# Backward pass of a sliding-window decode block on one Trainium2 core: 4 KB rows for two weight gradients, and three first loads on Pool's queue

## The chip, the cores and the metric

The kernel runs on one core of a Trainium2 chip. The metric is the time of one execution on the device in microseconds (us); of several runs the median is taken. A core has five engines that run their own instruction streams: PE (TensorE, matrix products and transposes), DVE (VectorE), ACT (ScalarE), POOL (GpSimd) and SP (SyncE, here only an issuer of transfers). Sixteen DMA engines move data between the chip's memory (HBM) and the core's working memory. A transfer is issued by SP or ACT through a hardware queue (q1 for SP, q10 for ACT in the profile), or by POOL through a software queue (q0).

## The reference

The forward function is y = x + attention(norm(x)) + ffn(norm(x)), and the kernel computes y and the gradients of it for a given grad_out. There are 4 sequences with one token each, D = 512.

```python
xn = layernorm(x)                                  # 4 x 1 x 512
q  = xn @ wq                                       # 32 heads of 128
k, v = k_cache[:, :, -1024:], v_cache[:, :, -1024:]  # 8 kv heads, 4 query heads share one
p  = softmax(q k^T / sqrt(128));  o = p v
y  = x + o @ wo + (gelu(xn @ w_gate) * (xn @ w_up)) @ w_down      # F = 1792
outputs: y, dx, dk_cache, dv_cache, dwq, dwo, dw_gate, dw_up, dw_down
```

The cache gradients have all 4096 positions, of which the first 3072 are zero: 50.3 MB of zeros are to be written beside 16.8 MB of dk and dv and 13.9 MB of weight gradients. Two of the outputs matter here: dwo = o^T grad_out (4096 x 512) and dwd = a^T grad_out (1792 x 512), with a the product of gelu and w_up's result. Both are sums over four rows only (the four sequences), so each is a matrix product with a very short inner dimension whose cost is in copying and storing the result. All arrays are bfloat16.

## The kernel before

The kernel has two parts in one instruction stream. The FFN part comes first: w_gate, w_up and w_down are loaded whole; xn and grad_out are transposed; the hidden values hg and hu are computed with xnT (L538 to L543); w_down is transposed on PE in seven steps and multiplied with grad_out to da (L582 to L589); a chain of small DVE operations gives a, dhg and dhu in transposed form; `f_rows` (L615) turns them back into rows (a_r, dhg_r, dhu_r); and the pieces of dwd (`piece_d`, L629), dw_gate and dw_up (`piece_g`, L640) are queued as background work.

The attention part then goes over NT = 4 groups t of two kv heads (eight query heads). `pre(t)` computes do and q of the group from wo and wq, `kv_steps` transposes k or v in eight steps and computes scores, `softmax` and `softmax_d` are chains of small operations whose links are placed between PE work, `odq` computes o (k = 0) and dq (k = 1), `dvdk` queues the pieces of dv and dk, `dw` those of dwo and dwq, and `fin` adds the group's part to y and dx.

The order is written out by hand. Each engine's instructions run in the order in which the program emits them. Background pieces stand in one queue, `bg`, and `tick(n)` emits the next n of them between other work; `link` does the same for the softmax chains. A copy from PE's result memory goes through `evac` (L89), which puts it on ACT or DVE by a running estimate of their load. A piece's last step emits its store on SP.

All stores, and k's and v's loads, are issued by SP, in program order. When SP reaches a store whose data is not ready, it waits, and everything behind it waits as well. The zeros of the cache gradients are stores of a zeroed tile, `ztile`, 1.5 MB each, 32 in all (`zero`, L161). They are placed between the other stores to keep the DMA engines fed: two after the first loads (L168), one after each dv or dk store (L478), single ones in the FFN part (L638, L650), and three ahead of the last group's dv (L706); what is left comes at the end (L727).

Before the change the first transfers are: ACT issues w_gate; SP issues x, grad_out, w_up, w_down (L150), wo and wq of group 0 (`load_w(0, nc.sync)`, L151), k and v of group 0, and then two zero stores. POOL builds the identity, sets `ztile` to zero (L167), builds `sel` (L177) and sets further tiles. POOL issues wo and wq of the later groups.

dwo is made as follows. `dym` (L232) holds grad_out spread by `spread_rows` (L234): four copies of it on 128 rows, in the i-th of which only the rows with row number i modulo 4 are kept. The product of the rows of o (one row for each sequence and query head) with the i-th copy is the block of dwo of query head i: 128 rows by 512. A staging tile holds four such blocks next to each other, and the store writes them as 128 x 4 rows of 512 elements, 1 KB each. dwd goes the same way with chunks of F in place of heads.

Of the kernel before, what the change touches and what calls it, by code (L numbers as in the profile page):

```python
# [9 lines left out]
ACT = mybir.ActivationFunctionType  # L10
ALU = mybir.AluOpType
AX = mybir.AxisListType
FP32 = mybir.dt.float32
BF16 = mybir.dt.bfloat16
P = 128
# [3 lines left out]
def kernel(  # L19
# [28 lines left out]
    nc = tc.nc  # L48

    B, Sq, D = A_x.shape  # L50
# [3 lines left out]
    rep = Hq // G  # L54
# [5 lines left out]
    GP = 2  # L60
# [56 lines left out]
    wo_t, wq_t, k_t, v_t = {}, {}, {}, {}  # L117
    w_pool, kv_pool = {0: w_a}, {0: kv_a}

    def load_w(t, eng=nc.gpsimd):  # L120
        pool = w_pool[t % 2]
        wo_t[t] = pool.tile([P, HG, D], BF16, name="wo_sb", tag="wo")
        eng.dma_start(out=wo_t[t][:], in_=wo_v[t])
        wq_t[t] = pool.tile([P, ND, CW], BF16, name="wq_sb", tag="wq")
        eng.dma_start(out=wq_t[t][:], in_=wq_v[t])

    def load_kv(t, k):
        if t >= NT:
# [18 lines left out]
    make_identity(nc, ident[:])  # L147

    wd_sb = ffn_w.tile([P, NF, D], BF16, name="wd_sb")
    nc.sync.dma_start(out=wd_sb[:], in_=B_w_down.rearrange("(c p) n -> p c n", p=P))  # L150
    load_w(0, nc.sync)  # L151
    for k in range(2):
        load_kv(0, k)

# [10 lines left out]


    nc.gpsimd.memset(ztile[:], 0.0)  # L167
    zero(2)  # L168
    ident_f = const.tile([P, P], FP32, name="ident_f")
    nc.vector.tensor_copy(out=ident_f[:], in_=ident[:])  # L170
# [58 lines left out]


    xnm = const.tile([P, rep, D], BF16, name="xnm")
    dym = const.tile([P, rep, D], BF16, name="dym")  # L232

    def spread_rows(src, dst):  # L234
        ps = ps_w.tile([P, D], FP32, name="row_ps", tag="w")
        nc.tensor.matmul(ps[:], lhsT=sel[:], rhs=src[:], start=True, stop=True)
        for i in range(rep):
            if i % 2:
                nc.scalar.activation(out=dst[:, i, :], in_=ps[:], func=ACT.Copy, scale=msk_i[:, i:i + 1])
            else:  # L240
                nc.vector.tensor_scalar(out=dst[:, i, :], in0=ps[:], scalar1=msk_i[:, i:i + 1], scalar2=None,
                                        op0=ALU.mult)
# [196 lines left out]
    def odq(t, k):  # L439
        pT, blks = st[t][("PT", "dST")[k]], (v_t, k_t)[k]  # L440
        cols = pT[:].rearrange("p j (y s) -> p j s y", s=SL)
        for j in range(JB):
            q, jj = j // JQ, j % JQ
            for g in range(GP):
                nc.tensor.matmul(od_ps[g * 32:g * 32 + B * rep, k, g, :], lhsT=cols[:, jj, g * NQ + q, :],  # L445
                                 rhs=blks[(t, g)][:, j, :], start=(j == 0), stop=(j == JB - 1),
                                 tile_position=(0, g * 32))
        rows = attw.tile([P, GP, Dh], BF16, name="od_r", tag=f"od_r{k}", bufs=2)
        if k == 0:
            nc.vector.tensor_copy(out=rows[:], in_=od_ps[:, k])  # L450
        else:
            nc.scalar.activation(out=rows[:], in_=od_ps[:, k], func=ACT.Copy, scale=scale)
        st[t][("o", "dq")[k]] = rows

    def odT(t, k):
        rows = st[t][("o", "dq")[k]]
# [27 lines left out]
        return made  # L484

    def dw(t):
        o_r, dq_r = st[t]["o"], st[t]["dq"]

        def piece_o(g, i, held):
            if i == 0:  # L490
                held["osb"] = outp.tile([P, rep, D], BF16, name="osb_o", tag="o")
            mps = ps_w.tile([P, D], FP32, name="dwo_ps", tag="w")
            nc.tensor.matmul(mps[:], lhsT=o_r[:, g, :], rhs=dym[:, i, :], start=True, stop=True)  # L493
            evac(held["osb"][:, i, :], mps[:], 512)
            if i == rep - 1:
                r0 = (t * HG + g * rep) * Dh
                store(nc.sync, out_5[r0:r0 + rep * Dh, :].rearrange("(h p) n -> p h n", p=P), held["osb"][:], "rest")

        def piece_q(c2, k, held):
            if k == 0:  # L500
                held["osb"] = outp.tile([P, 2, GP, rep, Dh], BF16, name="osb_q", tag="o")
            ci, i2 = k // 2, k % 2
            c = c2 * 2 + ci
            mps = ps_w.tile([P, 2, GP, Dh], FP32, name="dwq_ps", tag="w")
            for i in range(2):
                nc.tensor.matmul(mps[:, i].rearrange("p g d -> p (g d)"), lhsT=xnm[:, i2 * 2 + i, c * P:(c + 1) * P],  # L506
                                 rhs=dq_r[:].rearrange("p g d -> p (g d)"), start=True, stop=True)
            evac(held["osb"][:, ci, :, i2 * 2:(i2 + 1) * 2, :], mps[:].rearrange("p i g d -> p g i d"), 512)
            if k == 3:
                store(nc.sync, out_4[c2 * 2 * P:(c2 + 1) * 2 * P, t * CW:(t + 1) * CW].rearrange("(c p) j -> p c j", p=P),  # L510
                      held["osb"][:].rearrange("p c g i d -> p c (g i d)"), "rest")

        assert rep == 4
        made = []
        for g in range(GP):
            held = {}
            made.append([lambda g=g, i=i, held=held: piece_o(g, i, held) for i in range(rep)])
        for c2 in range(ND // 2):
            held = {}
            made.append([lambda c2=c2, k=k, held=held: piece_q(c2, k, held) for k in range(4)])  # L520
        return made
# [17 lines left out]
    for wi, wsb in enumerate((wg_sb, wu_sb)):  # L539
        for fc in range(NF):  # L540
            for c in range(ND):
                nc.tensor.matmul(hg_ps[:, wi, fc, :], lhsT=wsb[:, c, fc * P:(fc + 1) * P], rhs=xnT[:, c, :],
                                 start=(c == 0), stop=(c == ND - 1))  # L543
    spread_rows(dy4, dym)
    hgu = ffn.tile([P, 2, 4 * NF4, B], FP32, name="hgu")
    nc.gpsimd.memset(hgu[:], 0.0)
    nc.vector.tensor_copy(out=hgu[:, :, 0:NF], in_=hg_ps[:])
# [64 lines left out]
    nc.vector.tensor_tensor(out=dhg_f[:], in0=da[:], in1=hu, op=ALU.mult)  # L612
    nc.vector.tensor_tensor(out=by_chunk(dhgT_b), in0=fbi(dhg_f), in1=fbi(gp), op=ALU.mult)

    def f_rows(srcT, nm):  # L615

        ps = ps_w.tile([P, NF4, P], FP32, name="fr_ps", tag="w")
        for f4 in range(NF4):
            nc.tensor.matmul(ps[0:4 * B, f4, :], lhsT=srcT[:, f4].rearrange("p b i -> p (b i)"),
                             rhs=ident[:], start=True, stop=True)  # L620
        rows = const.tile([P, NF4, P], BF16, name=nm)
        nc.gpsimd.memset(rows[:], 0.0)
        evac(rows[0:4 * B], ps[0:4 * B], 512)
        return rows

    acc_sum(0, [(lambda c, fc=fc: wd_sb[:, fc, c * P:(c + 1) * P], aT_b[:, fc // 4, :, fc % 4]) for fc in range(NF)])
    a_r = f_rows(aT_b, "a_r")

    def piece_d(f4, i, n, held):  # L629
        if i == 0:  # L630
            held["osb"] = outp.tile([P, 4, D], BF16, name="osb_d", tag="o")
        mps = ps_w.tile([P, D], FP32, name="dwd_ps", tag="w")
        nc.tensor.matmul(mps[:], lhsT=a_r[:, f4, :], rhs=dym[:, i, :], start=True, stop=True)
        evac(held["osb"][:, i, :], mps[:], 512)
        if i == n - 1:
            store(nc.sync, out_8[4 * f4 * P:(4 * f4 + n) * P, :].rearrange("(h p) n -> p h n", p=P),
                  held["osb"][:, 0:n, :], "rest")
            zero(f4 == 1)  # L638

    def piece_g(s_r, og, c, i, held):  # L640
# [11 lines left out]
    for f4 in range(NF4):  # L652
        held = {}
        n = min(4, NF - 4 * f4)
        for i in range(n):
            bg.append(lambda f4=f4, i=i, n=n, held=held: piece_d(f4, i, n, held))
    df_ps = ps_a.tile([P, ND, B], FP32, name="df_ps", tag="S")
    edge = dict(lhsT=ztile[0:1, 0:P], rhs=ztile[0:1, 0:ND * B])
# [131 lines left out]
```

## Time and profile before

| What | Value |
|---|---|
| Runs | 285.17, 285.85, 285.30 us; median 285.3 |
| Profiled execution | 285.17 us, span of its instructions 283.4 us |
| TensorE clock granted, mean | 0.894 |
| PE, DVE, ACT, POOL busy | 201.9, 161.0, 116.9, 29.7 us |
| DMA packets | 23981, 112.12 MB, mean 396 GB/s |
| Read from and written to HBM | 30.68 and 81.01 MB |

The page of the profile gives busy time for each engine, the span in 40 slices with a digit for the busy share of each slice, the DMA queues with packets and bytes, the chain of waits that ended last, and the costliest groups of instructions. A row of a group or of the timeline reads: start and length in us, engine, line, operation, the tile written and the tiles read, their shapes, and in brackets how long the engine sat idle before and what ended that. SPq is SyncE's instruction stream. A DMA view can be asked for any stretch of time and then gives packets and bytes of each queue in it.

### The profile page before, as it was taken

What the parts mean: (1) busy time and instruction counts of PE and PEld (TensorE: products, weight loads), DVE (VectorE), ACT (ScalarE), POOL (GpSimd) and SP (SyncE); (2) the same over time, 40 slices, a digit from 0 to 9 for tenths busy, and PEclk for the clock granted to TensorE, in tenths of its full rate; (3) what the DMA queues carried; (4) which work ended last, traced back from release to release, by engine and by line L of the source; (5) the groups of instructions that cost most, each with busy time, mean ns of one, the idle gap of its engine ahead of it and who ended that gap; (6) DMA issues with size and microseconds to landing.
All of it is one profiled execution on the core that took longest, in us unless ns stands there. A gap on an engine that the chain in (4) does not pass through costs nothing.

```text
span 283.4 us, 6845 instructions
## 1 busy us (share of the span) xinstructions
PE 201.9 (71%) x2970; PEld 138.0 (49%) x2970; DVE 161.0 (57%) x310; ACT 116.9 (41%) x219; POOL 29.7 (10%) x32
## 2 busy tenths in 40 slices
PE   0455998898888799999894899999996997200000
PEld 0444676665556764676652567665555743100000
DVE  7756556476847555768562677667774387800000
ACT  2041484561146177644371564447660387200000
POOL 8400000043000700001600000220000000000000
PEclk9999599799999999999999599999997799955555
DMA  7999999999999999999999999999999979999993
GB/s 266 391 356 420 424 408 404 432 420 364 384 426 409 402 418 418 404 420 417 406 388 416 423 426 424 401 418 394 384 407 388 433 286 425 424 397 404 425 420 153
DMA packets 23981, 112.12 MB, mean 396 GB/s; under 512 B 1664, under 2 KB 10384, under 8 KB 15504
## 3 DMA queue, kind: packets, MB, share of 16 engines
q1 hardware_dynamic: 22160, 103.56, 90.4%
q0 software_dynamic: 1632, 6.29, 5.7%
q10 hardware_dynamic: 160, 1.84, 1.7%
q8 instruction: 23, 0.38, 0.5%
q14 instruction: 6, 0.05, 0.0%
HBM read 30.68 MB, written 81.01 MB: 394 GB/s over the span
## 4 chain that ended last, share of the span: by engine, by line
PE 34%; issue 19%; DMA 17%; DVE 10%; POOL 5%; ACT 3%; POOLq 0%; ACTq 0%; DVEq 0%; SPq 0%
DMA out_dram<-stg_dv 10%; DMA wq_sb<-in_A_wq_dram 7%; PE kv_ps L472 7%; PE T_ps L274 6%; PE od_ps L445 5%; PE S_ps L340 4%; PE dwq_ps L506 2%; DVE dS_s L362 2%; POOL ztile L167 2%; PE pT_ps L274 2%; PE dwo_ps L493 2%; DVE T_sb L98 1%; PE acc_ps L251 1%; DVE P_s L362 1%; PE woT_ps L274 1%
## 5 line engine op out<-in xcount | busy, mean ns | idle before, releaser
L98 DVE COPY T_sb<-T_ps 128x1024 bf16<-128x1024 bf16 x64 | 44.1, 689 | 25.3 <-PE T_ps L274 25.3
L97 ACT CAST stg_dv<-kv_ps 128x512 bf16<-128x512 f32 x52 | 28.4, 589 | 26.6 <-PE kv_ps L472 26.0
L97 ACT CAST stg_dk<-kv_ps 128x512 bf16<-128x512 f32 x51 | 28.4, 588 | 25.8 <-PE kv_ps L472 11.2
L472 PE MATMUL kv_ps<-qmr,dS_s 128*128 128x512 bf16 x64 | 22.9, 396 | 2.3 <-ACT stg_dk L97 1.4
L274 PE MATMUL T_ps<-ident,vb 128*128 128x128 bf16 x256 | 20.7, 228 | 4.6 <-ACT stg_dk L97 4.2
L324 POOL TENSOR_TENSOR domr<-r,msk 128x1024 bf16<-128x1024 bf16 x4 | 7.6, 1889 | 153.1 <-DVE r L321 126.3
L274 PEld LDWEIGHTS <-vb 128*128 128x128 bf16 x256 | 17.5, 102 | 9.1 <-issue 7.2
L472 PE MATMUL kv_ps<-domr,P_s 128*128 128x512 bf16 x64 | 21.6, 386 | 0.1
L274 PE MATMUL T_ps<-ident,kb 128*128 128x128 bf16 x256 | 19.5, 219 | 0.0
L274 PEld LDWEIGHTS <-kb 128*128 128x128 bf16 x256 | 16.5, 98 | 4.3 <-issue 0.9
L97 ACT CAST osb_q<-dwq_ps 128x512 bf16<-128x512 f32 x26 | 15.1, 586 | 7.2 <-PE dwq_ps L506 5.3
L97 ACT CAST osb_g<-dwg_ps 128x512 bf16<-128x512 f32 (+1 forms) x26 | 12.8, 538 | 10.0 <-PE dwg_ps L645 6.8
L97 ACT CAST osb_o<-dwo_ps 128x512 bf16<-128x512 f32 x24 | 13.8, 585 | 4.7 <-PE dwo_ps L493 3.8
L98 DVE COPY wgT<-wgT_ps 128x1024 bf16<-128x1024 bf16 x14 | 9.6, 689 | 7.9 <-PE wgT_ps L274 7.8
L98 DVE CAST stg_dv<-kv_ps 128x512 bf16<-128x512 f32 x12 | 8.2, 687 | 8.6 <-PE kv_ps L472 8.4
L340 PE MATMUL S_ps<-T_sb,qm 128*32 128x256 bf16 x128 | 12.7, 386 | 0.5 <-DVE T_sb L98 0.5
L98 DVE COPY woT<-woT_ps 128x1024 bf16<-128x1024 bf16 x16 | 11.0, 687 | 3.2 <-PE woT_ps L274 2.8
L340 PE MATMUL S_ps<-T_sb,dom 128*32 128x256 bf16 x128 | 12.7, 387 | 0.0
L98 DVE CAST stg_dk<-kv_ps 128x512 bf16<-128x512 f32 x13 | 8.6, 688 | 6.9 <-DMA out_dram<-stg_dv 5.8
L493 PE MATMUL dwo_ps<-dym,od_r 128*128 128x512 bf16 x32 | 11.9, 390 | 0.2
L506 PE MATMUL dwq_ps<-od_r,xnm 128*128 128x256 bf16 x64 | 11.8, 274 | 0.1
L98 DVE COPY wqT<-wqT_ps 128x1024 bf16<-128x1024 bf16 x16 | 10.6, 686 | 2.2 <-PE wqT_ps L274 2.1
(186 smaller groups left out, 363.9 us busy)
## 6 DMA issues: line engine op xcount, KB each, us to landing
out_dram<-ztile SPq DMA_DIRECT2D x32, 1536.0 KB, 18.6
kb<-in_A_k_cache_dram SPq DMA_DIRECT2D x8, 1024.0 KB, 13.4
vb<-in_A_v_cache_dram SPq DMA_DIRECT2D x8, 1024.0 KB, 18.6
out_dram<-stg_dv SPq DMA_DIRECT2D x8, 1024.0 KB, 15.5
out_dram<-stg_dk SPq DMA_DIRECT2D x8, 1024.0 KB, 16.1
out_dram<-osb_o SPq DMA_DIRECT2D x8, 512.0 KB, 19.2
out_dram<-osb_q SPq DMA_DIRECT2D x8, 512.0 KB, 11.9
out_dram<-osb_g SPq DMA_DIRECT2D x8, 448.0 KB, 8.5
```

Of the source, the lines that this page charges most:

```text
L97: return nc.scalar.copy(out=out, in_=in_)
L98: return nc.vector.tensor_copy(out=out, in_=in_)
L167: nc.gpsimd.memset(ztile[:], 0.0)
L251: nc.tensor.matmul(ps[:, c, :], lhsT=lf(c), rhs=rhs, start=(k == 0), stop=(k == len(terms) - 1))
L274: nc.tensor.transpose(ps[:, i, :], a, ident[:])
L324: nc.gpsimd.tensor_tensor(out=mr[:].rearrange("p g q d -> p (g q) d"), in0=r4[:, k, :].unsqueeze(1).broadcast_to([P, SL, Dh]), in1=msk[:]. ...
L340: nc.tensor.matmul(ps[b * RB:(b + 1) * RB, :], lhsT=zt[:, b * GP + g, c0:c0 + RB], rhs=T_sb[:].rearrange("p (x b) -> p b x", b=B)[:, b, :] ...
L362: nc.vector.scalar_tensor_tensor(out=out[:], in0=src[:].unsqueeze(2).broadcast_to([P, WQ, B]), scalar=rr[:, 0:1], in1=mskb[:].unsqueeze(1) ...
L445: nc.tensor.matmul(od_ps[g * 32:g * 32 + B * rep, k, g, :], lhsT=cols[:, jj, g * NQ + q, :], rhs=blks[(t, g)][:, j, :], start=(j == 0), st ...
L472: nc.tensor.matmul(mps[:].rearrange("p q d -> p (q d)"), lhsT=src[:, j * P:(j + 1) * P], rhs=mr[:, g].rearrange("p q d -> p (q d)"), start ...
L493: nc.tensor.matmul(mps[:], lhsT=o_r[:, g, :], rhs=dym[:, i, :], start=True, stop=True)
L506: nc.tensor.matmul(mps[:, i].rearrange("p g d -> p (g d)"), lhsT=xnm[:, i2 * 2 + i, c * P:(c + 1) * P], rhs=dq_r[:].rearrange("p g d -> p ...
```

## The change

The change has these parts.

- dwo: the four masked copies of grad_out are replaced by one unmasked, `dyr`. The mask goes to the other factor: after o of a group is there (`odq(t, 0)`), two POOL products write `o_s`, four copies of o's rows in which the i-th keeps the rows of head i. The product for step i then takes every fourth column of `o_s`, starting at i, so that its 128 result rows are the rows 4p + i of the 512 rows of dwo. With the four steps next to each other in the staging tile, a partition holds four rows of dwo that follow each other in HBM, and the store writes 128 rows of 4 KB.
- dwd: the same with `a_s` in place of `a_r`, made by `f_rows(..., spread=True)` in four masked copies that alternate between DVE and ACT. The last chunk of two blocks now takes four steps of 64 rows where it had two of 128: 16 products in place of 14.
- w_down is issued by POOL, behind the identity and ahead of the zeroing of `ztile`; wo and wq of group 0 are issued by POOL behind that zeroing. SP goes from w_up straight to k and v of group 0 and the two zero stores.
- POOL sets `a_s` to zero (128 x 2048) in place of `a_r` (128 x 512).

The zero stores keep their places in the program.

```diff
-    def load_w(t, eng=nc.gpsimd):
+    def load_w(t):
         ...
-        eng.dma_start(out=wo_t[t][:], in_=wo_v[t])
+        nc.gpsimd.dma_start(out=wo_t[t][:], in_=wo_v[t])
         ...
-        eng.dma_start(out=wq_t[t][:], in_=wq_v[t])
+        nc.gpsimd.dma_start(out=wq_t[t][:], in_=wq_v[t])
...
-    nc.sync.dma_start(out=wd_sb[:], in_=B_w_down.rearrange("(c p) n -> p c n", p=P))
-    load_w(0, nc.sync)
+    nc.gpsimd.dma_start(out=wd_sb[:], in_=B_w_down.rearrange("(c p) n -> p c n", p=P))
     for k in range(2):
         load_kv(0, k)
...
     nc.gpsimd.memset(ztile[:], 0.0)
+    load_w(0)
     zero(2)
...
-    dym = const.tile([P, rep, D], BF16, name="dym")
-
-    def spread_rows(src, dst):
+    dyr = const.tile([P, D], BF16, name="dyr")
+    msk_r = const.tile([P, rep], BF16, name="msk_r")
+    nc.vector.tensor_copy(out=msk_r[:], in_=msk_i[:])
+
+    def spread_rows(src, dst, masked=True):
         ps = ps_w.tile([P, D], FP32, name="row_ps", tag="w")
         nc.tensor.matmul(ps[:], lhsT=sel[:], rhs=src[:], start=True, stop=True)
+        if not masked:
+            evac(dst[:], ps[:], 512)
+            return
...
         st[t][("o", "dq")[k]] = rows
+        if k == 0:
+            o_s = attw.tile([P, GP, rep, Dh], BF16, name="o_s", tag="o_s", bufs=2)
+            for g in range(GP):
+                nc.gpsimd.tensor_tensor(out=o_s[:, g], in0=rows[:, g].unsqueeze(1).broadcast_to([P, rep, Dh]),
+                                        in1=msk_r[:].unsqueeze(2).broadcast_to([P, rep, Dh]), op=ALU.mult)
+            st[t]["os"] = o_s
...
-            nc.tensor.matmul(mps[:], lhsT=o_r[:, g, :], rhs=dym[:, i, :], start=True, stop=True)
+            nc.tensor.matmul(mps[:], lhsT=o_s[:, g].rearrange("p r d -> p (r d)")[:, i:rep * Dh:rep], rhs=dyr[:],
+                             start=True, stop=True)
...
-                store(nc.sync, out_5[r0:r0 + rep * Dh, :].rearrange("(h p) n -> p h n", p=P), held["osb"][:], "rest")
+                store(nc.sync, out_5[r0:r0 + rep * Dh, :].rearrange("(p i) n -> p (i n)", i=rep),
+                      held["osb"][:].rearrange("p i n -> p (i n)"), "rest")
...
-    spread_rows(dy4, dym)
+    spread_rows(dy4, dyr, masked=False)
...
-    def f_rows(srcT, nm):
+    def f_rows(srcT, nm, spread=False):
         ...
+        if spread:
+            rows = ffn.tile([P, NF4, 4, P], BF16, name=nm)
+            nc.gpsimd.memset(rows[:], 0.0)
+            for i in range(4):
+                if i % 2:
+                    nc.scalar.activation(out=rows[0:4 * B, :, i, :], in_=ps[0:4 * B], func=ACT.Copy,
+                                         scale=msk_i[0:4 * B, i:i + 1])
+                else:
+                    nc.vector.tensor_scalar(out=rows[0:4 * B, :, i, :], in0=ps[0:4 * B],
+                                            scalar1=msk_i[0:4 * B, i:i + 1], scalar2=None, op0=ALU.mult)
+            return rows
...
-    a_r = f_rows(aT_b, "a_r")
+    a_s = f_rows(aT_b, "a_s", spread=True)
...
+        m = n * P // 4
         mps = ps_w.tile([P, D], FP32, name="dwd_ps", tag="w")
-        nc.tensor.matmul(mps[:], lhsT=a_r[:, f4, :], rhs=dym[:, i, :], start=True, stop=True)
-        evac(held["osb"][:, i, :], mps[:], 512)
-        if i == n - 1:
-            store(nc.sync, out_8[4 * f4 * P:(4 * f4 + n) * P, :].rearrange("(h p) n -> p h n", p=P),
-                  held["osb"][:, 0:n, :], "rest")
+        nc.tensor.matmul(mps[0:m], lhsT=a_s[:, f4].rearrange("p i f -> p (i f)")[:, i:n * P:4], rhs=dyr[:],
+                         start=True, stop=True)
+        evac(held["osb"][0:m, i, :], mps[0:m], 512)
+        if i == 3:
+            store(nc.sync, out_8[4 * f4 * P:(4 * f4 + n) * P, :].rearrange("(p i) n -> p (i n)", i=4),
+                  held["osb"][0:m].rearrange("p i n -> p (i n)"), "rest")
             zero(f4 == 1)
...
-        for i in range(n):
+        for i in range(4):
             bg.append(lambda f4=f4, i=i, n=n, held=held: piece_d(f4, i, n, held))
```

More of the change, by code (lines that the diff above doesn't have):

```diff
@@ L486, in dw @@
     def dw(t):
-        o_r, dq_r = st[t]["o"], st[t]["dq"]
+        o_s, dq_r = st[t]["os"], st[t]["dq"]
         def piece_o(g, i, held):
```

## The prediction

> **What bounds the kernel now.** I read the page first, for what the DMA engines do, then the queues' rows for single stretches of time, then SyncE's own waits and the timeline of the first 45 us, because most of the change lies there, and last the chain.
>
> Four lines of the page:
>
> ```profile
> DMA  7999999999999999999999999999999979999993
> DMA packets 23981, 112.12 MB, mean 396 GB/s; under 512 B 1664, under 2 KB 10384, under 8 KB 15504
> q1 hardware_dynamic: 22160, 103.56, 90.4%
> q0 software_dynamic: 1632, 6.29, 5.7%
> ```
>
> The DMA engines are busy from the second slice to the last, with one dip (the slice with a 7, around 229 us) and a slow start. 112 MB have to be moved whatever the order, so the time is the bytes' own time plus every microsecond in which the queue is empty. A compute engine counts only where its lateness empties the queue. q0, the queue of Pool's transfers, moved 6.29 MB in 5.7% of 283.4 us, which is 389 GB/s; its 4 KB packets are the only ones of that size in this trace.
>
> The DMA view of three stretches, 13 to 17 us (only 1 KB rows of w_down and wo), 24 to 30 us (only 8 KB rows of k and v), and 69 to 72.5 us (Pool's wo beside k and v):
>
> ```profile
> DMA packets 1380, 1.40 MB, mean 350 GB/s; under 512 B 13, under 2 KB 1380, under 8 KB 1380
> ...
> DMA packets 353, 2.50 MB, mean 417 GB/s; under 512 B 44, under 2 KB 44, under 8 KB 50
> ...
> q1 hardware_dynamic: 124, 0.89, 66.0%
> q0 software_dynamic: 109, 0.45, 36.2%
> ```
>
> Rows of 1 KB move at 350 GB/s, rows of 8 KB at 417. In the third stretch 0.89 MB of 8 KB rows are 109 packets, and q0 has 109 of 4 KB (0.45 MB): the two queues take turns packet by packet, so Pool's queue gets a third of the bandwidth beside 8 KB rows.
>
> SyncE's waits, and the timeline rows of PE, SyncE and ScalarE that decide the start:
>
> ```profile
> SPq L103 <- ACT osb_d L97: 16.5, 4, 13.7
> 18.00 1.89 PE L274 MATMUL wdT_ps<-ident,wd_sb 128*128 128x128 bf16 x16 [2.98 <-DMA wd_sb<-in_B_w_down_dram]
> 19.09 1.27 SPq L103 DMA_DIRECT2D out_dram<-ztile  x2
> 31.18 0.57 ACT L97 CAST a_r<-fr_ps 16x512 bf16<-16x512 f32 x1 [2.29 <-PE fr_ps L619]
> 36.11 2.88 SPq L103 DMA_DIRECT2D out_dram<-osb_d  x2
> ```
>
> PE starts w_down's transposes when w_down lands, at 18.0. SyncE, after two zero stores at 19.1, stands 13.7 us at the first dwd store. Until then the engines live on what was queued: loads of 11.8 MB (w_gate, w_up and w_down 1.84 each, wo and wq 1.05 each, k and v 4.19) and 3.1 MB of zeros. 1 KB rows of dwd first appear between 39 and 40 us, where the rate falls to 333 GB/s from 419 in the three microseconds before. So the queued work ends at about 39.4, 3.3 us after the store was issued: a small margin.
>
> The chain, where it goes through a DMA:
>
> ```profile
> 65.43 19.51 DMA wq_sb<-in_A_wq_dram
> 136.44 19.60 DMA out_dram<-stg_dv
> 228.26 8.36 DMA out_dram<-stg_dv
> ```
>
> Twice compute waits some 20 us for a DMA, which is a queue full of older work. A queue that is late by some time at 85 or 156 us hands its lateness to compute. The third comes after the dip: there compute was late and the queue empty.
>
> **The change, part by part.** The sum is made against the profiled execution, 285.17 us with a span of 283.4; the median of the runs is 285.3, 0.13 higher.
>
> Larger packets. dwd (1.84 MB) and dwo (4.19 MB) go from 1 KB to 4 KB rows on the hardware queue. No such packet is in the trace: 389 GB/s (4 KB on q0) and 417 (8 KB) are the ends, I take 400. From 350, dwd saves 1.84/350 - 1.84/400 = 0.65 us, dwo 1.49 (0.37 a group); the ends are 1.7 and 2.8 for both. w_down and the first wo (2.88 MB) go from 350 to q0's 389: 0.84. wq moved at 388 between 20 and 22 us: 0. Together 3.0 us of DMA time. The Trainium skill, "DMA: Bandwidth & Descriptors" (Why small descriptors are slow), has a fixed overhead of about 3 cycles a packet beside a 32 B beat, from which I estimate 35 beats for 1 KB and 131 for 4 KB, a saving of 6.4%, or 1.6 us on these 8.9 MB. The trace's own rates, 350 against 389 to 417, differ by more, and the sum goes by them.
>
> w_down on Pool. Pool issues it after the identity, at 1.4 us. Its issue with 1792 rows is not shown; wo's (1024 rows) took 0.93 to 1.06 and wq's (512) 0.76, so 1.2 to 1.5. q0 has no packet until 68.9 for an issue begun at 64.4, 4.5 us; so w_down's first packets come at about 6.3. At that time w_gate and w_up, done at 11.3 before, have 5.0 us to go: 9.4 rows of 14 KB for each engine, 0.536 each, 7.5 of them w_up's. In turns, 7.5 of w_down's 28 packets for each engine (0.168 at 389 GB/s) go meanwhile, to 12.6. The other 20.5 take turns with 8 KB rows of k and v, which now follow w_up at once on SyncE's queue (0.314 + 0.168 = 0.482 a turn): 9.9 us, to 22.5. Before, the data was through at 16.5 (11.3 + 1.84/350) and w_down landed at 18.0; the same 1.5 puts landing at 24.0, 6.0 later. Ends: 18 if q0 starts at once and its share beside w_gate and w_up is larger than a turn, 25.5 if some engine lags. The Trainium skill speaks against this edit in the same page's rules: transfers from several issuing engines share the same 16 DMA engines and interleave, so spreading them saves issue time alone. The 109 to 109 packets agree with the interleaving; by the rule the move is worth nothing in bandwidth.
>
> SyncE's queue loses three loads; wo and wq held it 8.61 and 3.57 us there. k, v and the two zeros are issued earlier (zeros at about 8, when Pool's memset of 5.2 us, now behind w_down's issue, ends). All of that lies in a full queue: 0. Pool's later memsets move from 6.5 to about 10, and that of a_s is longer (four times the 0.51 of a_r); PE needs sel at 14.4 before and later now, a_s past 31: 0 while Pool isn't held.
>
> dyr. One copy takes the place of four masked ones that ran one after another (15.06 to 18.04): 2.3 us saved, but then comes the wait for w_down: 0.
>
> a_s. Four copies that alternate between VectorE and ScalarE, some 3.0 us by the dym rows, in place of 0.57. PE's first dwd product, at 32.48, can start at about 34.1: +1.6 on the path to the first store. dwd has 16 products instead of 14; two more of 0.38 and their copies of 0.59 fall behind that store.
>
> o_s. Two Pool products of 128x512 a group; 128x1024 took 1.89, so 0.95 each. Pool is idle for over 25 us before each group's domr, and dwo comes after dk: 0 for themselves. But VectorE's dS_s reads SBUF twice about then (215.72, after od_r at 214.68), and VectorE's identity cast took 5.2 us beside Pool's memset of 5.2. Between 0 and 1.7 us on compute, over two groups after 156; I take 0.8. PE waits longer for w_down; after the half idle slice at 149 to 156 us its clock fell to 0.55 in the next one (a 5 in the page's PEclk row), so w_down's transposes may run slower: 0 to 2 us, left at 0, since the 18.1 us taken from before hold a slow stretch too (clock 0.55 in the slice from 28.3 to 35.4). Weights read in steps of four: the nearest row, L445's stepped weights, loads in 107 ns against 98 for L274: 0.
>
> Sum. Queued work ends at 39.4 - 0.84 = 38.6. First dwd data: 24.0 + 18.1 (from landing to store issue before) + 1.6 + 1.1 (issue to data, as at 228.26) = 44.8. The queue stands empty 6.2 us, and 0.9 more between the first two dwd stores, which are ready 2.2 apart (four copies) and drain in 1.3: 7.1. Less 0.84, 0.65 and 0.37 (first group's dwo), the queue is 5.2 late at 156, and compute with it. From there compute sets the store at 228.26: +0.8, and what dwo saves between goes into a longer dip. The last group's dwo gives 0.37 back. 285.2 + 5.2 + 0.8 - 0.4 = 290.8.
>
> **The rivals.** First, other side: w_down lands early enough. For it: only w_gate and w_up stand beside it at first, and Pool issues it at 1.4. Against it: the turns at 69 us. The queue does not run dry if w_down lands by 38.6 - 20.8 = 17.8; then 0.84, 0.65 and twice 0.37 are earned against 0.8 for o_s, 283.8, and 282.2 if o_s costs nothing and the dip passes all 3.0 on. It decides from a landing near 18.3 (empty for 1.4 us in all, what is earned less o_s); each microsecond later costs one.
>
> Second: Pool is held at the issue of wo or wq until w_down has drained, as SyncE was for 8.61 us at wo. Then sel comes at 23 or later, ahead of w_down's transposes on PE, and the dry stretch grows by 2 to 5: 293 to 296. Against it: 1536 rows were issued by Pool at 64.4 without a hold; 3328 are asked for now.
>
> Third: lateness is swallowed, because less waiting for output buffers (2.8 us of ScalarE on dwd's stores at 50) lets compute catch up and the queue has little to do. The bytes remain, so I see at most half of it: 286 to 288.
>
> **How the numbers follow.** Forecast and its neighbourhood (287 to 294) 0.61; w_down early 0.17, nearly all of it faster; Pool held 0.11; swallowed 0.11, a part of it within 0.3%, which is 0.9 us and about what this kernel's runs can tell from no change. Faster 0.16, same 0.05, slower 0.79. The range takes in an early landing with part of its gain, 283.2, and a late one with o_s at its upper end, 295.5; the forecast's own range is 287.5 to 294.
>
> **What would show it.** The DMA row of 38 to 45 us nearly empty; w_down's transposes starting at 22 to 26 instead of 18; SyncE's wait for osb_d well over 20 us; q0 with 1.84 + 2.1 MB more; packets under 2 KB fewer by 8,700. Wrong if w_down lands before 20, if the stretch around 40 us stays full, or if the dip near 229 takes up the lateness.

## The result, and the profile after

The changed kernel takes 292.8 us (median of four runs, 291.57 to 294.25) against 285.2 before: a ratio of 1.026, 95% interval 1.021 to 1.031. It is slower by 7.6 us where 5.5 were forecast. The profiled execution took 292.91 us, with a span of 291.1.

The page of the changed kernel, the DMA part (busy tenths in 40 slices of 7.3 us, packets, and the two queues):

```profile
DMA  7999936999999999999999999999999979999991
DMA packets 17197, 112.12 MB, mean 385 GB/s; under 512 B 1664, under 2 KB 1680, under 8 KB 8720
...
q1 hardware_dynamic: 14368, 99.63, 83.7%
q0 software_dynamic: 2640, 10.22, 8.9%
```

The same 112.12 MB move in fewer packets: 8,704 fewer under 2 KB, as the row sizes say, and q0 has gone from 6.29 to 10.22 MB. New is a hole, the 3 and the 6 in the sixth and seventh slice, from 36 to 51 us. The windows of that stretch (start and end, length, busy time and instructions of PE, PE's weight loads, DVE, ACT and POOL, then the granted TensorE clock, the DMA share and GB/s):

```profile
36.00:40.00 4.00, 3.08 (x53) 2.35 (x50) 2.83 (x10) 0.84 (x2) 0.00 (x0) 0.50 0.72 303
40.00:44.00 4.00, 3.34 (x26) 2.27 (x27) 1.09 (x2) 3.00 (x6) 0.00 (x0) 0.50 0.02 9
44.00:46.00 2.00, 2.00 (x32) 1.48 (x30) 0.89 (x2) 1.30 (x3) 0.00 (x0) 0.76 0.49 184
46.00:62.00 16.00, 15.74 (x263) 12.06 (x260) 11.07 (x19) 11.88 (x23) 0.00 (x0) 1.00 0.90 351
```

From 40 to 44 us sixteen engines move 9 GB/s. Over 36 to 62 us the missing shares add up to 4 x 0.28 + 4 x 0.98 + 2 x 0.51 + 16 x 0.10 = 7.7 us. Nearly all of it lies between 38 and 48 us, where the share is 0.25, so that 7.5 us are missing. Before, the same stretch was full but for parts of single microseconds; the weakest between 36 and 48 us and the two behind it:

```profile
39.00:40.00 1.00, 1.00 (x21) 0.76 (x19) 0.61 (x2) 0.99 (x3) 0.00 (x0) 1.00 0.85 333
40.00:41.00 1.00, 1.00 (x19) 0.70 (x16) 0.61 (x2) 0.99 (x3) 0.00 (x0) 1.00 1.03 369
41.00:42.00 1.00, 1.00 (x14) 0.77 (x14) 0.25 (x2) 0.82 (x2) 0.00 (x0) 1.00 1.11 399
```

What empties the queue is told by the timeline rows and SyncE's wait (us in all, times, longest):

```profile
1.52 1.26 POOL L150 DMA_DIRECT2D wd_sb<-in_B_w_down_dram  x1
2.77 5.24 POOL L166 MEMSET ztile<- 128x6144 bf16 x1
7.93 0.89 POOL L123 DMA_DIRECT2D wo_sb<-in_A_wo_dram  x1
24.50 1.89 PE L279 MATMUL wdT_ps<-ident,wd_sb 128*128 128x128 bf16 x16 [7.76 <-DMA wd_sb<-in_B_w_down_dram]
39.84 0.68 ACT L641 ACTIVATE a_s<-fr_ps,msk_i 16x512 bf16<-16x512 f32 x1 [0.81 <-DVE a_s L644]
40.66 1.01 PE L660 MATMUL dwd_ps<-dyr,a_s 128*128 128x512 bf16 x2 [1.58 <-ACT a_s L641]
44.25 3.22 SPq L103 DMA_DIRECT2D out_dram<-osb_d  x2
```

```profile
SPq L103 <- ACT osb_d L97: 38.5, 4, 32.1
```

POOL issues w_down at 1.52, half a microsecond before SyncE did (1.99), and yet PE's transposes of it start at 24.50 instead of 18.00, after 7.76 us idle. Everything up to the first dwd store follows: that store is issued at 44.25 instead of 36.11. SyncE stands 32.1 us at it (13.7 before). All that stands behind it waits as well, the next zero store too, whose data is ready, while what was queued ran out at about 38.6.

How the lateness travels is seen by asking both traces when the same number of bytes had moved. Before, up to 60 and 111 us:

```profile
DMA packets 7367, 23.27 MB, mean 388 GB/s; under 512 B 348, under 2 KB 4964, under 8 KB 5957
...
DMA packets 10617, 43.96 MB, mean 396 GB/s; under 512 B 660, under 2 KB 5276, under 8 KB 7611
```

After, up to 67.4 and 120 us:

```profile
DMA packets 3624, 23.20 MB, mean 344 GB/s; under 512 B 342, under 2 KB 350, under 8 KB 2212
...
DMA packets 7007, 44.01 MB, mean 367 GB/s; under 512 B 657, under 2 KB 665, under 8 KB 4054
```

At equal bytes, 23.2 MB are through 7.6 us later than before (67.4 instead of 59.8) and 44 MB 8.8 us later. 95 MB are through 6.9 us later (244.6 instead of 237.7), behind the dip of each kernel. So the lateness is that of the hole, some 1.2 us more are lost between 67 and 120 us in a queue that isn't empty, and about 1.9 are won back later. The chain of waits hands the lateness to compute, with its DMA links in their old places:

```profile
70.56 19.45 DMA wq_sb<-in_A_wq_dram
139.89 23.70 DMA out_dram<-stg_dv
235.18 8.70 DMA out_dram<-stg_dv
```

They started at 65.43, 136.44 and 228.26 before; compute reaches the last one 6.9 us late, and the span ends 7.7 us late.

### The profile page after: what moved, and what is told of

Its sections match the earlier page's. It is cut to its first block, busy times and chain, and to the rows that moved or that the text cites. A ratio compares the mean times of both kernels' runs of the same rounds, so it can differ in the third digit from the quotient of the medians.

```text
span 291.1 us, 6868 instructions
## 1 busy us (share of the span) xinstructions
PE 200.5 (69%) x2972; PEld 137.1 (47%) x2972; DVE 162.4 (56%) x313; ACT 117.6 (40%) x219; POOL 42.7 (15%) x43
## 2 busy tenths in 40 slices
DMA packets 17197, 112.12 MB, mean 385 GB/s; under 512 B 1664, under 2 KB 1680, under 8 KB 8720
## 3 DMA queue, kind: packets, MB, share of 16 engines
q0 software_dynamic: 2640, 10.22, 8.9%
## 4 chain that ended last, share of the span: by engine, by line
PE 30%; issue 20%; DMA 18%; DVE 12%; POOL 6%; ACT 2%; DVEq 0%; POOLq 0%; SPq 0%; ACTq 0%
DMA out_dram<-stg_dv 11%; DMA wq_sb<-in_A_wq_dram 7%; PE kv_ps L484 5%; PE T_ps L279 5%; PE od_ps L450 4%; PE S_ps L345 4%; PE dwq_ps L520 3%; DVE dS_s L367 2%; DVE T_sb L98 2%; POOL ztile L166 2%; PE dwo_ps L505 2%; DVE wqT L98 2%; PE pT_ps L279 1%; PE acc_ps L256 1%; DVE P_s L367 1%
## 5 line engine op out<-in xcount | busy, mean ns | idle before, releaser
L463 POOL TENSOR_TENSOR o_s<-od_r,msk_r 128x512 bf16<-128x512 bf16 x8 | 9.1, 1159 | 109.3 <-DVE od_r L455 80.0
L98 DVE CAST stg_dk<-kv_ps 128x512 bf16<-128x512 f32 x12 | 7.9, 687 | 10.1 <-DMA out_dram<-stg_dv 9.5
L520 PE MATMUL dwq_ps<-od_r,xnm 128*128 128x256 bf16 x64 | 12.5, 299 | 0.1
L505 PE MATMUL dwo_ps<-dyr,o_s 128*128 128x512 bf16 x32 | 12.3, 404 | 0.5 <-DVE stg_dk L98 0.2
## 6 DMA issues: line engine op xcount, KB each, us to landing
out_dram<-ztile SPq DMA_DIRECT2D x32, 1536.0 KB, 17.8
out_dram<-stg_dv SPq DMA_DIRECT2D x8, 1024.0 KB, 17.8
```

What stands on the lines that cost most here:

```text
L98: return nc.vector.tensor_copy(out=out, in_=in_)
L463: nc.gpsimd.tensor_tensor(out=o_s[:, g], in0=rows[:, g].unsqueeze(1).broadcast_to([P, rep, Dh]), in1=msk_r[:].unsqueeze(2).broadcast_to([P ...
L505: nc.tensor.matmul(mps[:], lhsT=o_s[:, g].rearrange("p r d -> p (r d)")[:, i:rep * Dh:rep], rhs=dyr[:], start=True, stop=True)
```

## The experiments

The theory: w_down, moved to POOL's queue, shares the engines packet by packet with everything on SyncE's queue, lands 6.5 us later, and the queue runs dry before the first dwd store; the larger rows earn a little. Rivals: the rows and their copies (`a_s`, `o_s`) cost the time themselves; compute's lateness costs it, full queue or not; POOL's issue is what is late. A ratio is against the kernel before on the same chip, with its 95% interval; 0.001 is 0.29 us.

**The moved loads alone.** The kernel before, with only the loads moved.

```diff
-    nc.sync.dma_start(out=wd_sb[:], in_=B_w_down.rearrange("(c p) n -> p c n", p=P))
-    load_w(0, nc.sync)
+    nc.gpsimd.dma_start(out=wd_sb[:], in_=B_w_down.rearrange("(c p) n -> p c n", p=P))
...
     nc.gpsimd.memset(ztile[:], 0.0)
+    load_w(0)
```

> The kernel before with one part of the change alone: w_down and the first wo and wq issued by Pool at the change's places; dwo, dwd, dym and a_r as before. Theory A (the change is slower because w_down, taking turns with k and v, lands late and the DMA queue runs empty before the first dwd store): w_down lands at 24 to 24.5 us, the first dwd store is issued 18.1 later, at about 42.3 (before 36.1, after 44.3), the queue is empty from about 39 to 43.5, and the time is 289 to 291. Rival B (the cost is in the 4 KB rows and what they need: o_s on Pool beside dS_s, four copies for a_s, stepped weights): 284.5 to 285.5, since the loads alone cost nothing.

291.4 us, ratio 1.0224 [1.0188, 1.0261]: 6.4 us (5.4 to 7.4) of the 7.6, a little above the 289 to 291 expected. Its timeline and its windows:

```profile
24.98 1.89 PE L274 MATMUL wdT_ps<-ident,wd_sb 128*128 128x128 bf16 x16 [7.50 <-DMA wd_sb<-in_B_w_down_dram]
...
43.48 0.43 SPq L103 DMA_DIRECT2D out_dram<-osb_d  x1
```

```profile
36.00:38.00 2.00, 1.73 (x58) 1.72 (x59) 1.79 (x11) 0.24 (x1) 0.00 (x0) 0.50 1.02 422
38.00:44.00 6.00, 6.00 (x55) 4.29 (x54) 1.91 (x5) 3.41 (x7) 0.00 (x0) 0.53 0.30 122
44.00:46.00 2.00, 2.00 (x37) 1.53 (x34) 1.17 (x3) 2.00 (x4) 0.00 (x0) 1.00 0.76 254
```

With the old rows, w_down is as late and the hole is there again: 6 x 0.70 + 2 x 0.24 = 4.7 us up to 46 us, 5.7 between 38 and 48, where the changed kernel has 7.5. The loads carry most of the loss.

**The rows alone.** The changed kernel with the three loads back on SyncE in their old order.

```diff
-    nc.gpsimd.dma_start(out=wd_sb[:], in_=B_w_down.rearrange("(c p) n -> p c n", p=P))
+    nc.sync.dma_start(out=wd_sb[:], in_=B_w_down.rearrange("(c p) n -> p c n", p=P))
+    load_w(0, nc.sync)
...
-    load_w(0)
```

> The changed kernel with its loads put back: w_down, wo and wq of group 0 on SyncE's queue where they were before; 4 KB rows, o_s, a_s and dyr stay. A: w_down lands at 18, the first dwd store goes out at about 37.7 and its data moves from 38.8, before the queue has drained (39.4), so no empty stretch around 40 us; the saved DMA time of dwo (0.4 a group) is earned less some 0.6 for dS_s: 283 to 284.8. B: 290 or more.

285.42 us, 1.0028 [1.0013, 1.0043]: a miss. The rows alone win nothing; they lose 0.8 us. w_down is there at 17.83 again, but the first dwd store comes at 38.20 instead of 36.11, mostly because of the copies of `a_s` (1.7 us in the changed kernel), and the small margin that before had is gone. Windows of this kernel:

```profile
40.00:41.00 1.00, 1.00 (x21) 0.77 (x19) 0.67 (x1) 0.98 (x3) 0.00 (x0) 1.00 0.50 193
41.00:42.00 1.00, 1.00 (x20) 0.76 (x18) 0.60 (x2) 0.98 (x3) 0.00 (x0) 1.00 0.65 262
49.00:50.00 1.00, 1.00 (x19) 0.84 (x18) 0.35 (x1) 0.73 (x2) 0.00 (x0) 1.00 0.41 156
```

These three microseconds alone lack 1.4 us of engine time (0.50 + 0.35 + 0.59).

**The hole filled.** The changed kernel with two more zero stores, which have to be made anyway, ahead of the first dwd store.

```diff
-    zero(2)
+    zero(4)
```

> The changed kernel with four zero stores behind the first loads in place of two, so that two of the five last ones move to the front; the number of bytes is the same. A: w_down still lands at about 24.5 and the first dwd store is still issued at about 44.3, but the queue now holds 3.1 MB more, 7.4 us, and lasts to about 46: no empty stretch. The time falls by nearly all of it, to 284 to 287, although compute stays as late as in the changed kernel. B: compute's lateness is what costs, and the time stays at 291 to 293.

284.99 us, 1.0021 [1.0007, 1.0034]. In its timeline w_down and the first store are as late as in the changed kernel, and in its windows the engines are full up to 46 us:

```profile
24.20 1.89 PE L279 MATMUL wdT_ps<-ident,wd_sb 128*128 128x128 bf16 x16 [7.03 <-DMA wd_sb<-in_B_w_down_dram]
...
44.47 0.38 SPq L103 DMA_DIRECT2D out_dram<-osb_d  x1
```

```profile
38.00:44.00 6.00, 4.42 (x36) 2.88 (x34) 2.57 (x4) 3.62 (x7) 0.00 (x0) 0.50 1.02 431
44.00:46.00 2.00, 2.00 (x22) 1.44 (x20) 0.69 (x1) 1.25 (x3) 0.00 (x0) 0.50 0.96 408
```

Compute is 8 us late at the first store, and all but 0.6 us of the loss is gone; from 46 to 50 us the engines still lack 1.0 us (4 us at a share of 0.74). Compute stays late to the end: the last dv store that it waits for is issued at 236.24 instead of 228.26. But three zero stores are left behind it instead of five, so as many bytes are through at the end as before. The lateness of compute costs next to nothing by itself; the empty queue is what costs.

**Only wo and wq on POOL.** The changed kernel with w_down on SyncE again, behind w_up.

```diff
-    nc.gpsimd.dma_start(out=wd_sb[:], in_=B_w_down.rearrange("(c p) n -> p c n", p=P))
+    nc.sync.dma_start(out=wd_sb[:], in_=B_w_down.rearrange("(c p) n -> p c n", p=P))
```

> The changed kernel with w_down alone put back on SyncE's queue, behind w_up and ahead of k and v; wo and wq of group 0 stay on Pool. If queues take turns packet by packet, w_down's 112 rows of 1 KB for each engine stand turn by turn beside wo's and wq's 32 packets of 4 KB (0.168 us each), 5.4 us of them: w_down lands at about 23, nearly as late as on Pool, and the time is 290 to 292.5. If it is Pool's queue as such that is slow, or bytes are shared evenly, w_down lands at 18 to 20 and the time is 283 to 286.

292.34 us, 1.0274 [1.0253, 1.0295]: no better, as the turns have it, though w_down is later than the 23 us expected. Its timeline:

```profile
24.28 1.89 PE L279 MATMUL wdT_ps<-ident,wd_sb 128*128 128x128 bf16 x16 [8.72 <-DMA wd_sb<-in_B_w_down_dram]
...
44.02 0.36 SPq L103 DMA_DIRECT2D out_dram<-osb_d  x1
```

w_down is now on the queue it had before, right behind w_up, and it still lands 6.3 us late. What differs for it is that wo and wq, which nothing needs yet, no longer stand behind it but beside it, in q0's 4 KB packets against its rows of 1 KB. Between 10 and 17 us q0 has 410 packets (1.61 MB) and SyncE's queue 422 (0.96 MB). So it isn't POOL's issue that is late. A queue beside the urgent one is enough.

**Smaller packets beside w_down.** The changed kernel with the first group's k and v in two halves each, rows of 4 KB in place of 8.

```diff
-            nc.sync.dma_start(out=tl[:].rearrange("p j d -> p (j d)"),
-                              in_=src[:, t * GP + g, K0:Sk, :].rearrange("b (m j) d -> m b (j d)", j=JB))
+            for j0 in ((0, JB // 2) if t == 0 else (0,)):
+                jn = JB // 2 if t == 0 else JB
+                nc.sync.dma_start(out=tl[:, j0:j0 + jn, :].rearrange("p j d -> p (j d)"),
+                                  in_=src[:, t * GP + g, K0:Sk, :].rearrange("b (m j) d -> m b j d", j=JB)
+                                  [:, :, j0:j0 + jn, :].rearrange("m b j d -> m b (j d)"))
```

> The changed kernel with the loads of the first group's k and v split into halves of each row: eight transfers with rows of 4 KB in place of four with rows of 8 KB, the same bytes in the same place of SyncE's queue. If w_down is late because the queues take turns packet by packet, a turn beside k and v now takes 0.168 + 0.168 us in place of 0.314 + 0.168: w_down's last 20.5 turns take 6.9 us instead of 9.9, it lands at 21 to 22 in place of 24.5, the empty stretch shrinks by 2.5 to 3 and the time is 289 to 290.5. If Pool's queue has a rate of its own (some 130 GB/s), w_down still lands at 24 to 25 and the time is 291.5 to 293.5.

289.4 us, 1.0166 [1.0145, 1.0188]. Its timeline:

```profile
21.95 1.89 PE L282 MATMUL wdT_ps<-ident,wd_sb 128*128 128x128 bf16 x16 [5.46 <-DMA wd_sb<-in_B_w_down_dram]
...
41.69 3.26 SPq L103 DMA_DIRECT2D out_dram<-osb_d  x2
```

The same bytes are queued beside w_down, in packets half as long, and it lands 2.55 us earlier than in the changed kernel; the first store comes 2.56 earlier and the run is 2.8 us shorter (1.0264 - 1.0166). The packets of the two queues between 17 and 24 us in the changed kernel:

```profile
q1 hardware_dynamic: 248, 1.82, 65.6%
q0 software_dynamic: 250, 0.96, 34.4%
```

With the halved rows it is 368 (1.36 MB) beside 370 (1.45 MB) in the same time. A turn belongs to a packet, at 1, 4 and 8 KB.

The hole between 38 and 48 us and the loss go together over these kernels: 7.5 us and 7.6 in the changed kernel, 6.8 and 7.8 with w_down on SyncE, 5.7 and 6.4 with the loads alone, 4.6 and 4.7 with halved rows, 0.4 and 0.6 with four zeros.

**The rows, with cover.** The second experiment's kernel with a third zero store ahead of the first dwd store.

```diff
-    zero(2)
+    zero(3)
```

> The rows-only kernel (4 KB rows, loads as before) with three zero stores behind the first loads in place of two. Theory: rows alone came out at 285.4 against 284.6 because a_s's four copies put the first dwd store at 38.2, and the engines were half empty from 40 to 42 and again near 49, some 2 us; a third zero store (3.7 us of transfer) covers that: 283.0 to 284.2. If what the rows need (o_s, a_s, 16 products) costs by being on compute's path, it stays at 285 to 285.8.

283.21 us, 0.9951 [0.9935, 0.9967]. Windows:

```profile
40.00:41.00 1.00, 1.00 (x20) 0.76 (x18) 0.69 (x1) 0.65 (x2) 0.00 (x0) 1.00 0.96 397
41.00:42.00 1.00, 1.00 (x20) 0.76 (x18) 0.69 (x1) 0.98 (x3) 0.00 (x0) 1.00 1.06 442
49.00:50.00 1.00, 0.74 (x14) 0.50 (x11) 0.90 (x2) 0.00 (x0) 0.00 (x0) 1.00 1.00 414
```

The three half-empty microseconds are full, and the rows are worth 1.4 us: less than the 2.14 put down for them, with the sign that was forecast. This version is faster than both kernels, and than the one before by 0.5%.

**dwo's rows without dwd's.** dwd is made as before, from `a_r` and the masked `dym`, which is kept beside `dyr`; the loads are on SyncE and two zeros stand ahead. Against the second experiment:

```diff
+    dym = ffn.tile([P, rep, D], BF16, name="dym")
...
-    spread_rows(dy4, dyr, masked=False)
+    spread_rows(dy4, dym, plain=dyr)
...
-    a_s = f_rows(aT_b, "a_s", spread=True)
+    a_r = f_rows(aT_b, "a_r")
...
-        nc.tensor.matmul(mps[0:m], lhsT=a_s[:, f4].rearrange("p i f -> p (i f)")[:, i:n * P:4], rhs=dyr[:],
-                         start=True, stop=True)
+        nc.tensor.matmul(mps[:], lhsT=a_r[:, f4, :], rhs=dym[:, i, :], start=True, stop=True)
```

> Only dwo by 4 KB rows (o_s on Pool, dyr beside dym); dwd with dym and a_r as before, loads as before. Theory: without a_s the first dwd store is issued at 36 to 37, ahead of the queue's end, so there is no empty stretch; dwo's rows save 0.4 us a group, and dS_s gives back some 0.6: 283.2 to 284.2. If o_s costs as much as the rows save: 284.4 to 285.3.

283.92 us, 0.9978 [0.9967, 0.9989]: 0.6 us won. So dwd's part of the change is what turned the rows into a loss.

**The same with a third zero.**

```diff
-    zero(2)
+    zero(3)
```

> As the kernel with dwo's rows alone, with three zero stores behind the first loads. If the queue does not run dry there any more, the third zero does nothing: within 0.4 us of the kernel with two. If it is faster by 0.8 or more, the queue still ran dry in the FFN part.

283.23 us, 0.9950 [0.9933, 0.9968]. That is 0.7 us faster than with two, between the two values that would have decided, and equal to the version with dwd's rows too: the means of the six runs of each lie 0.1 us apart, with some 0.5 us of uncertainty. With the queue full, dwd's rows are worth nothing that can be measured at the end.

**Is it the third zero alone?** The kernel before with nothing but `zero(3)` in place of `zero(2)`.

> The kernel before, with three zero stores ahead of the first dwd store in place of two, and nothing else changed. If the gain of the versions with three zeros comes from the larger rows, with the zero as mere cover, then this is the same as before within 0.3% (284.0 to 285.6 where before is 284.8), because before has no stretch at 40 us in which its DMA engines stand empty (rate 333 GB/s in the worst single microsecond there). If the third zero by itself is worth what it was worth in the pair of versions with dwo's rows alone, 0.7 us, this is 284.1 or below where before is 284.8, ratio 0.9975 or lower.

284.62 us, 0.9998 [0.9987, 1.0008]: the same as before. So the third zero alone doesn't make the gain of the versions with three zeros; it comes with dwo's rows, and the zero is cover. Why it is worth 0.7 us to the version with dwo's rows alone, whose queue was nearly full around 40 us already, and nothing here, isn't settled.

**o_s away from POOL.** The version with the rows and three zeros, with `o_s` made by four ACT copies in place of two POOL products.

```diff
-            for g in range(GP):
-                nc.gpsimd.tensor_tensor(out=o_s[:, g], in0=rows[:, g].unsqueeze(1).broadcast_to([P, rep, Dh]),
-                                        in1=msk_r[:].unsqueeze(2).broadcast_to([P, rep, Dh]), op=ALU.mult)
+            for r in range(rep):
+                nc.scalar.activation(out=o_s[:, :, r, :], in_=rows[:], func=ACT.Copy, scale=msk_i[:, r:r + 1])
```

> The rows kernel with three first zeros (283.2 us), with o_s written by ScalarE (four copies of 128x256 a group, scaled by the mask) in place of two Pool products. If Pool's products cost by holding up VectorE's dS_s (1.47 in the middle and 1.68 at most in the changed kernel, 1.285 before), dS_s is back at 1.285 in all four groups and the time falls by 0.2 to 0.7; ScalarE has room for four copies of about 0.4. If the collision costs nothing at the end: within 0.3 of 283.2.

283.26 us, 0.9944 [0.9922, 0.9965], against 0.9951 [0.9935, 0.9967] with POOL: 0.2 us apart, with some 0.8 of uncertainty. DVE's `dS_s` (duration in ns: lowest, median, highest) in the version with POOL's product and then in this one:

```profile
L367 DVE SCALAR_TENSOR_TENSOR dS_s<-Gt,rr,mskb x4: 1285/1640/1679, 86.1 to 218.4; 128x1024 bf16<-128x1024 f32 x4
```

```profile
L367 DVE SCALAR_TENSOR_TENSOR dS_s<-Gt,rr,mskb x4: 1283/1285/1286, 86.7 to 218.3; 128x1024 bf16<-128x1024 f32 x4
```

The collision is there, some 0.4 us for each group that has it, it goes away with POOL's product, and the end doesn't move by anything that these runs can tell.

**No transfer on POOL's queue at all.** The kernel before, the changed one and the versions with three zeros end with some microseconds in which the DMA share is 0.06 or 0.07, as much as one engine of sixteen (the trace doesn't tell which engine a packet was on). The idea was that POOL's queue leaves one engine behind. The later wo and wq go to SyncE, in the version with all rows and in the one with dwo's alone (three zeros in both).

```diff
-        load_w(1)
+        load_w(1, nc.sync)
...
-                load_w(t + 2)
+                load_w(t + 2, nc.sync)
```

> The rows kernel with three first zeros (283.2 us), with the later groups' wo and wq issued by SyncE too, so that no transfer goes through Pool's queue. In all kernels so far one sixteenth of the engines' time (a share of 0.06) is all that moves in the last 3 to 6 us: one engine is behind. If it falls behind through Pool's queue, the last 3 us go and the time is 280 to 282. If that engine is behind for another reason, the tail stays, and since 1 KB rows take the place of 4 KB packets for wo (some 0.4 us a group), the time is 283 to 285.

> The same edit to the kernel with dwo's rows alone and three first zeros (283.2 us), where the stretch with a share of 0.06 is longest, 273 to 279 us. If the engine falls behind through Pool's queue: 277.5 to 280.5. If not: 283 to 285.

284.04 us, 0.9972 [0.9955, 0.9989], and 285.43 us, 1.0004 [0.9988, 1.0021]: 0.6 and 1.5 us slower than with POOL's queue, the second a little above the 283 to 285 expected. The last windows of the first:

```profile
274.00:277.00 3.00, 0.00 (x0) 0.00 (x0) 0.00 (x0) 0.00 (x0) 0.00 (x0) 0.50 0.69 291
277.00:280.00 3.00, 0.00 (x0) 0.00 (x0) 0.00 (x0) 0.00 (x0) 0.00 (x0) 0.50 0.07 29
```

The tail is still there without POOL's queue, so the idea fell as it was put: POOL's queue isn't needed for it. In the second version the tail is gone, and the run is slower; its engines stood partly idle between 200 and 220 us, and again from 228 to 236:

```profile
200.00:210.00 10.00, 9.71 (x101) 5.35 (x99) 7.48 (x15) 6.35 (x12) 0.00 (x0) 1.00 0.86 350
210.00:220.00 10.00, 9.29 (x141) 6.42 (x139) 7.07 (x13) 5.90 (x12) 0.00 (x0) 1.00 0.92 371
...
228.00:236.00 8.00, 7.99 (x128) 5.66 (x125) 4.37 (x10) 4.66 (x9) 0.00 (x0) 0.86 0.62 256
```

## Why the prediction was right, and where it was off

**The landing of w_down**, the step that the forecast hung on, was worked out as 24.0 us from turns of one packet each; PE started on it at 24.50. q0's first packets were put at 6.3 and came at 6.8; POOL's issue of w_down took 1.26 us (1.2 to 1.5). The two experiments on it, wo and wq alone on q0 and halved rows of k and v, moved the landing as packet turns say. The Trainium skill, "DMA: Bandwidth & Descriptors" (Issuing engines are not separate DMA queues), says that transfers of all issuing engines run on the same sixteen DMA engines and interleave; the runs agree, and show that here the interleaving cost 6.4 us.

**The queue running dry.** The queued work was to end at 38.6 and did; the first dwd store was to be issued at 43.7 (44.25), its data to come at 44.8 (45.1), the engines to stand empty for 7.1 us in all (7.5). The extra 1.6 us for `a_s` were 1.7: from w_down's transposes to the first dwd product 16.16 us instead of 14.48. The copies alternate between two engines, but each waits for the one before (the bracket of the row at 39.84), so alternating saved nothing. The experiment with four zeros shows that this hole, not compute's lateness, is the loss.

**What the larger rows earn** was put at 3.0 us of DMA time. The page's shares give 98.3% of 283.4 = 278.6 us of busy engines before and 95.0% of 291.1 = 276.5 after: 2.1 saved. The term that was mis-sized is dwd's 0.65, as far as the end goes: with the queue covered, the versions with and without dwd's larger rows are 0.9951 and 0.9950. The engines did save it. In the packet records of these two traces dwd's 1,792 rows of 1 KB take 5.1 us of all sixteen engines, its 448 rows of 4 KB 4.5. Why it doesn't reach the end is open. In the changed kernel dwd's packets come right behind the hole, when stores are fed one by one as they get ready, so faster packets would only lengthen the wait for the next ones; in the covered version the later first store may eat the gain. Both are argued, not shown. dwo's rows did what was said, 1.4 us with cover (0.9 to 1.9), against 1.49. Whether the 0.84 for w_down and wo on POOL's queue was earned isn't shown: when 14 MB are through, the changed kernel is 0.8 us ahead of before, but so are the rows alone by 0.7, and the loads alone not at all.

**Lateness in between.** The forecast had the queue 5.2 us late at 156 and compute with it; compute was 7.5 late there (the store of dwo behind that wait is issued at 163.66 instead of 156.12). Of these 2.3 us, 0.65 are dwd's term and 0.4 the longer hole. The rest, about 1.2, was lost behind the hole in queues that weren't empty, which no step of the forecast had. At equal bytes the lateness grew from 6.6 us right behind the hole (15.55 MB, at 48 us instead of 41.4) to 7.6 at 23.2 MB and 8.8 at 44 MB. From 23.2 to 44 MB it also grew by 0.8 us with the loads alone moved, by 2.0 with four zeros, by 0.1 with the rows alone and by 0.7 with the rows and three zeros, so no single part of the change is shown to make it. A part lies in one stretch: from 72 to 82 us, where q0's load of the second group runs beside stores of dw_gate, engines 97% busy moved 327 GB/s; the stretch that answers to it before, 65 to 75 us, had 361 at a share of 1.00. Why is open.

**o_s** was given 0.8 us of compute (from 0 to 1.7). `dS_s` took up to 1.68 us instead of 1.285 beside it, and `o_s` 1.04 and at most 2.02 instead of 0.95, but the run with `o_s` on ACT is no faster beyond its uncertainty, so no cost at the end is shown. Compute's lateness fell from 7.5 at 156 to 6.9 at the last dv store instead of growing.

**The end.** The last group's dwo was to give back 0.4; the end is 0.8 later than that dv store instead. When 112.05 MB are through, at 279 before and 286 after, the difference is 7.0 us; the remaining 0.7 lies behind, in the tail. So the sum was low by 2: 0.65 for dwd, 0.4 for the hole, 1.2 for what was lost behind it, and 1.2 for the end, less 0.8 for `o_s` and the 0.6 by which compute's lateness fell (the dip near 235 us lacks 1.4 us of engine time, the one near 229 lacked 2.0). That the number is this near is in part luck, since terms of 3.4 on one side met 1.4 on the other; the landing, the hole and its size were worked out. The upper end of the range, 295.5, isn't what the two terms named for it give, 290.8 + 1.5 + 0.9 = 293.2.

**The rivals.** An early landing fell at 24.50 against 17.8. POOL held at wo or wq fell: the two were issued at 7.93 and 8.81 in 0.89 and 0.76 us. Swallowed lateness fell, too: 7.5 us of hole arrived as 7.7. The price of the first rival was wrong as well. It was given 283.8, or 282.2 at best, for a landing at 17.8. The second experiment, with its loads on SyncE, has this landing (17.83) without the 0.84 for faster loads, which leaves a gain of 0.6 of that price. It took 285.42, a loss of 0.8: its first store is issued at 38.20, but the engines are half empty between this store and the next. The forecast had that gap, 0.9 us, in its own sum and left it out of the rival's.

## What to carry to other kernels

In a kernel bound by its transfers, find the first store that depends on compute and ask what keeps the queue fed until then; two zero stores moved there were worth 7 us, and the gain of all the larger rows showed only with such a cover (1.4 us against a loss of 0.8). In this case a load that is needed first did best with nothing less urgent on a second queue: such loads shared the engines with it packet by packet, and small rows lost against large ones. Time saved in the engines isn't yet time saved at the end (dwd's larger rows: 0.6 us against nothing that could be measured), so ask of each store what stands behind it before costing it.

## What the runs showed of the hardware

- Here two queues shared the engines by packets and not by bytes: 248 packets of 1.82 MB beside 250 of 0.96 MB in 7 us. The same megabytes beside w_down in packets half as long let it land at 21.95 instead of 24.50 us, and its 1 KB rows beside 4 KB packets at 24.28 instead of 18.00.
- In most of these kernels the transfers end with about 3 us at a share of 0.06 or 0.07, as much as one engine of sixteen. Before, 279 to 282 us; the changed kernel, 286 to 289; dwo's rows with three zeros, two windows from 273 to 279:

```profile
279.00:282.00 3.00, 0.00 (x0) 0.00 (x0) 0.00 (x0) 0.00 (x0) 0.00 (x0) 0.50 0.06 25
```

```profile
286.00:289.00 3.00, 0.00 (x0) 0.00 (x0) 0.00 (x0) 0.00 (x0) 0.00 (x0) 0.50 0.06 25
```

```profile
273.00:276.00 3.00, 0.00 (x0) 0.00 (x0) 0.00 (x0) 0.00 (x0) 0.00 (x0) 0.50 0.12 49
276.00:279.00 3.00, 0.00 (x0) 0.00 (x0) 0.00 (x0) 0.00 (x0) 0.00 (x0) 0.50 0.07 29
```

  In the last of them 110.81 of 112.12 MB were through at 270 us, and the span ended at 280.7: some 6 us of the end have the share of two engines or of one. The tail remained in one of the two kernels without POOL's queue and was gone in the other. What makes it is open.
- A POOL product with two inputs in SBUF beside DVE's `dS_s` made that one longer by up to 0.39 us (1.285 to 1.679); with the same values made by ACT it stayed at 1.286.
